# A long convolution and an MLP in one program: four token tiles' first statistics from a second copy of x, and a new total order

## The chip, the cores and the metric

The program runs on one core of one Trainium2 chip. The metric is the device time of one execution in microseconds (us), as the median of several runs. Engines are named as the profile names them: PE (matrix multiply; PEld its weight loads), DVE (vector), ACT (scalar and activations), POOL (GpSimd), SP (sync, which issues most DMAs).

## The reference, cut to what matters

x is `A_q`, 2048 tokens by 640 channels in bf16. All norms are without weights.

```python
h  = x + A(_layernorm(x), k, v, shift_k, ssm_k, ssm_D)
h2 = h + mish(_layernorm(h) @ w1 + b1) @ w2          # w1: 640x1728, w2: 1728x640
# A(q, k, v, ...):
k_shift = causal convolution of k with 4 taps (shift_k), channel by channel
kv = k_shift * v
y  = irfft(rfft(kv, 2S) * rfft(ssm_k, 2S))[:S] + kv * ssm_D
A  = q * y
```

So per channel there is a convolution of length 2048 with a filter of length 2048 (`ssm_k`, one row a channel), whose result is multiplied by the first norm of x and added to x; then a second norm and an MLP with the Mish activation.

## The kernel before, in words

The convolution is a Fourier transform in two stages of matmuls with constant tables. Channels go in 5 groups of 128 (`dc` 0 to 4), tokens in 16 tiles of 128 (`t` 0 to 15). Every step is a small operation object with a name, an engine and its dependencies (`OP`, and `load` for a DMA on SP). Nothing is ordered by a scheduler: the long string `ORDER` lists every operation once, and `_ordered` puts them out in that order, so each engine gets its own operations in the order in which the string has them, and each engine runs its list strictly from first to last. `name@2` gives the PSUM slot (there are four of 128x1024 f32) that a PE operation writes; `:d`, `:p`, `:a` puts an operation on DVE, POOL or ACT instead of its first choice. An operation on PE can start only when the slot's earlier tile was read.

The stages, with the names used in `ORDER` and the profile's lines:

- Filter. `d_n0` to `d_n4` load `ssm_k` (512 KB each, line 328) into the upper part of the big buffer `ks`, from column 20480 on (`raw_n`). `dadd` adds `ssm_D` to the first tap, `k1pe` transposes on PE (L379), `k1ev` copies out of PSUM (L264 on ACT, L266 on DVE: the helper `ev`). `s1kpe` is the first transform stage of the filter (L399, L400; 20 tiles) and `s1kev` the copy out.
- Shift of k. `d_k` loads k; `ktpe` transposes it (L344), `ktev` copies out, `ktsh` shifts a copy on POOL (L348). `d_sk` loads the shift taps (5 KB) by a DMA that ACT issues (L273), `cfpe` spreads them over the partitions with one matmul (L307), `coef` copies that out on DVE (L312), `wsh` makes banded weights of it on POOL (L320), and `kspe` applies them (L360, L361; 10 tiles). `kv` multiplies with v on DVE (L365).
- `s2kpe`, `s2kev` (22 tiles, L425): second stage of the filter, which needs all of `s1kev`. `sw` swaps halves by ten DMAs within `ks` (L453): they write the upper half of `ks`.
- `s1vpe`, `s1vev` (20 tiles), `s2v..pe`, `s2v..ev` (20 tiles): the same two stages for kv. `pr` (20 on DVE, L464) multiplies the spectra. `i1pe`, `i1ev` (20 tiles, L485): first inverse stage. All copies out of PSUM here are casts of 128x1024 or 128x960 on ACT or DVE.
- Per token tile: `i2` (L537) is the last inverse stage, `y` its copy out; `d_x0` to `d_x3` load x into `rb`, where v was; `ln1_t` is the first norm's statistics on DVE (two BATCH_NORM_STATS2 of 320 elements, L516, and an aggregate, L517), `ln1p` the inverse root on POOL, `lnx` the normalised tile; `wb` and `h` multiply and add; `bn`, `pow`, `hc`, `tr` are the second norm and its transposes.
- `m1pe` (L604, L611), `hb` (L626), `m2pe` (L669, L677), `res` (L694), `d_out`: the MLP in five units of tokens.

The x load `d_x` waits for `kv`, since it overwrites v; the statistics wait for `d_x`:

```python
d_x = [load(f"d_x{i}", rb[:, 4 * i * D:4 * (i + 1) * D], ..., deps=[kv_ops[m, i // 2] for m in range(NDC)]) for i in range(4)]
o_ls = OP(f"ln1_{t}", "dve", [d_x[t // 4]], emit=ln1)
cf_pe = OP("cfpe", "pe", [d_cst, d_sk], psum=cf_p, ...)
```

Of the kernel before, what the change touches and what calls it, by code (L numbers as in the profile page):

```python
# [18 lines left out]
D = 640  # L19
# [7 lines left out]
d_dr wz idn d_n0 cz wm@0 small lane d_n1 d_cst d_sk d_n2 warm d_n3 d_n4 d_g0 dsel dcol dadd0 d_k2 k1pe0@1 d_k3 dadd1:p k1pe1@2 d_a12 k1ev0b d_k0 k1ev0  # L27
s1kpe0_3@3 k1ev1 s1kpe0_1@0 s1kev0_3 d_k1 s1kpe0_0@1 dadd2 s1kev0_1 s1kpe1_3@2 s1kev0_0:d dadd3:p d_g4 s1kpe0_2@3 k1pe2@0 s1kev0_2 dadd4:p d_g1
s1kev1_3 kz b1pe@1 k1pe4@3 k1ev2 c_b1 cfpe@2 k1pe3@1 k1ev4:a coef d_v0 s1kpe2_0@0 k1ev3 wsh1 s1kpe2_1@2 s1kev2_0 s1kpe4_3@3 d_g7 s1kev2_1:d s1kpe3_1@1
s1kev4_3 s1kpe2_2@0 wsh3 s1kpe1_0@2 s1kev3_1 d_v1 s1kev2_2:d s1kpe4_1@3 d_g2 s1kev1_0 s1kpe3_2@1 s1kev4_1:d s1kpe1_2@0 s1kev3_2 d_g6 ktpe0_0@2 wsh2  # L30
ktpe0_3 ktpe0_2 s1kev1_2 ktpe2_0@3 ktpe2_3 ktpe2_2 d_v2 ktpe2_1 ktpe0_1 ktev2 ktpe1_0@1 ktev0:a ktpe1_1 ktpe1_3 ktpe1_2 s1kpe3_3@0 d_g5 ktev1 ktsh2
s1kpe4_0@3 s1kev3_3 s1kpe1_1@2 ktsh0 s1kev4_0:d d_v3 s1kpe4_2@1 wsh0 s1kev1_1 s1kpe3_0@0 s1kev4_2:d s1kpe2_3@3 s1kev3_0 d_g3 ktpe4_0@2 ktpe4_2 ktpe4_3
s1kev2_3 ktsh1 ktpe3_0@1 ktpe4_1 ktpe3_3 ktev4 ktpe3_1 ktpe3_2 s2kpe_6@0 s2kpe_12@3 ktev3 s2kev_6 kspe0_0@2 s2kev_12 s2kpe_18@0 kv0_0 ktsh3 kspe2_0@1
s2kev_18 ktsh4 s2kpe_42@3 kv2_0 kspe3_0@2 s2kev_42 s2kpe_96@0 kv3_0 s2kpe_24@1 s2kev_96 kspe4_0@3 s2kev_24 kspe1_0@2 kv4_0 s2kpe_108@0 kspe1_1@1 kv1_0
# [24 lines left out]
d_out5 hb4_3 d_out6 m2pe8@0 m1pe4_0@3 hb4_6 m2pe11@1 hb4_0 res11 m2pe12@3 d_out4 m2pe14@1 res9 m2pe10@2 res12 m2pe13@3 res14 res13 d_out12 d_out14
res10 m2pe15a@1 m2pe15b@3 d_out9 d_out13 d_out10 d_out11 res15a res8 d_out15a res15b d_out8 d_out15b  # L60
# [112 lines left out]
def kernel(  # L173
# [14 lines left out]
    nc = tc.nc  # L188
# [551 lines left out]
```

## Time and profile before

| | |
|---|---|
| median of 3 runs | 222.97 us (222.88 to 223.0) |
| the profiled execution | 223.02 us |
| its span, first to last instruction | 221.2 us, granted PE clock 0.999 |
| busy in the span | PE 212.5 us, DVE 137.6 us, ACT 127.9 us, POOL 62.0 us |

The span is 1.82 us shorter than the profiled execution's own time. Shares over the whole span mix stages with different limits here, so the span is best read in stretches: the filter and the shift of k (to about 28 us), the second stage of the filter between the shift's matmuls (to about 45 us), the transforms of kv and the products (to about 89 us), the first tiles of the last inverse stage (to about 97 us), and the MLP.

### The profile page before, as it was taken

To read this page: it belongs to the slowest core of one execution; us is meant where nothing else is said; L and a number is where in the kernel's file an instruction comes from. 1 tells how busy PE (TensorE), PEld (TensorE's weight loads), DVE (VectorE), ACT (ScalarE), POOL (GpSimd) and SP (SyncE) were. 2 spreads that over 40 slices of the span, in tenths; PEclk is the share of its full clock that TensorE was granted. 3 is DMA by queue.
4 is the path that set the end of the run, shared out by engine and by line. 5 is a ranking of instruction groups with operands and counts; after the bars stand their busy time and mean duration, and the time that the engine had idled before them with its cause. 6 is when DMAs were issued, how large, how long until landed. Compare 5 with 4: busy or idle time off the path is not lost.

```text
span 221.2 us, 6309 instructions
## 1 busy us (share of the span) xinstructions
PE 212.5 (96%) x2740; PEld 156.0 (71%) x2746; DVE 137.6 (62%) x236; ACT 127.9 (58%) x175; POOL 62.0 (28%) x123
## 2 busy tenths in 40 slices
PE   7899999999879999999999999999999999999994
PEld 2899999898769998578867644444567445667663
DVE  2776899999999999899998679920002200002223
ACT  2389888999999999899753038426600257020000
POOL 5147620011870002147988655320000000000000
PEclk9999999999999999999999999999999999999999
DMA  5999994462992690833004402552001100000204
GB/s 168 393 408 416 407 403 109 166 205 87 410 409 92 207 384 9 276 127 77 0 1 27 94 0 59 124 119 59 0 3 59 59 0 3 0 0 3 89 0 148
DMA packets 19564, 30.98 MB, mean 140 GB/s; under 512 B 10705, under 2 KB 14929, under 8 KB 18769
## 3 DMA queue, kind: packets, MB, share of 16 engines
q1 hardware_dynamic: 19104, 30.46, 40.0%
q8 instruction: 21, 0.34, 0.6%
q10 hardware_dynamic: 336, 0.12, 0.2%
q14 instruction: 7, 0.05, 0.1%
q0 software_dynamic: 96, 0.00, 0.0%
HBM read 20.42 MB, written 2.62 MB: 104 GB/s over the span
## 4 chain that ended last, share of the span: by engine, by line
PE 72%; ACT 12%; DVE 6%; DMA 5%; issue 2%; SPq 1%; DVEq 0%; ACTq 0%
PE ps L669 26%; PE ps L604 26%; ACT uv L264 9%; PE ps L537 3%; DMA ks<-ks 3%; PE ps L399 3%; PE ps L425 3%; DMA ks<-in_A_ssm_k_dram 3%; PE ps L344 2%; PE ps L379 2%; DVE ks L266 2%; ACT ks L264 2%; PE ps L360 2%; DVE ra L365 1%; DVE uv L266 1%
## 5 line engine op out<-in xcount | busy, mean ns | idle before, releaser
L626 ACT ACTIVATE ks<-ps,b1s 128x512 bf16<-128x512 f32 (+1 forms) x69 | 36.2, 599 | 44.1 <-PE ps L604 35.1
L669 PE MATMUL ps<-ks 128*128 128x320 bf16 (+2 forms) x420 | 58.6, 299 | 0.0
L604 PE MATMUL ps<-G 128*128 128x512 bf16 (+1 forms) x319 | 57.2, 336 | 0.3
L669 PEld LDWEIGHTS <-ks 128*128 128x128 bf16 x420 | 40.6, 98 | 17.4 <-issue 1.3
L694 DVE TENSOR_TENSOR rb<-ps,rb 128x640 bf16<-128x640 f32 x15 | 11.8, 817 | 64.5 <-PE ps L677 52.2
L604 PEld LDWEIGHTS <-G 128*128 128x128 bf16 x325 | 31.4, 98 | 24.3 <-issue 1.1
L264 ACT CAST ks<-ps 128x960 bf16<-128x960 f32 (+3 forms) x48 | 39.3, 896 | 8.3 <-PE ps L400 5.0
L264 ACT CAST uv<-ps 128x1024 bf16<-128x1024 f32 x46 | 42.6, 1157 | 0.5 <-PE ps L485 0.4
L464 DVE TENSOR_TENSOR ks<-ks,uv 128x2048 bf16<-128x2048 bf16 x20 | 23.4, 1236 | 0.2 <-DMA ks<-ks 0.2
L425 PEld LDWEIGHTS <-G 128*128 128x128 bf16 x512 | 21.0, 96 | 3.1 <-issue 2.5
L485 PE MATMUL ps<-a_t,ks 128*128 128x128 bf16 (+1 forms) x416 | 17.1, 208 | 0.4
L485 PEld LDWEIGHTS <-ks 128*128 128x128 bf16 (+1 forms) x416 | 16.5, 114 | 1.0 <-issue 0.4
L266 DVE CAST uv<-ps 128x1024 bf16<-128x1024 f32 x14 | 16.4, 1210 | 0.2
L530 POOL TENSOR_SCALAR ra<-rb,r,nmr 128x640 bf16<-128x640 bf16 x11 | 12.5, 1133 | 9.9 <-PE ps L400 9.3
L425 PE MATMUL ps<-uv,G 128*128 128x64 bf16 (+1 forms) x384 | 12.9, 187 | 1.7 <-ACT uv L264 1.5
L550 DVE BATCH_NORM_STATS2 st<-rb 128x6 f32<-128x320 bf16 x32 | 14.0, 479 | 0.1
L516 DVE BATCH_NORM_STATS2 st<-rb 128x6 f32<-128x320 bf16 x32 | 13.7, 469 | 0.0
L365 DVE TENSOR_TENSOR ra<-ps,rb 128x1024 bf16<-128x1024 f32 x10 | 11.9, 1222 | 0.7 <-PE ps L361 0.5
L266 DVE CAST ks<-ps 128x1024 bf16<-128x1024 f32 (+2 forms) x10 | 11.3, 1160 | 1.0 <-PE ps L537 0.6
L528 ACT ACTIVATE ra<-rb,nmr,r 128x640 bf16<-128x640 bf16 x5 | 4.5, 925 | 11.9 <-POOL nmr L523 11.9
L425 PE MATMUL ps<-ks,G 128*128 128x160 bf16 x128 | 11.2, 230 | 0.1
L399 PE MATMUL ps<-cst,ra 128*64 128x128 bf16 x160 | 10.6, 219 | 0.7 <-ACT uv L264 0.5
(71 smaller groups left out, 252.7 us busy)
## 6 DMA issues: line engine op xcount, KB each, us to landing
ks<-ks SPq DMA_DIRECT2D x10, 512.0 KB, 6.3
G<-tab_g SPq DMA_DIRECT2D x8, 512.0 KB, 11.1
ks<-in_A_ssm_k_dram SPq DMA_DIRECT2D x5, 512.0 KB, 6.5
ra<-in_A_k_dram SPq DMA_DIRECT2D x4, 640.0 KB, 10.6
rb<-in_A_v_dram SPq DMA_DIRECT2D x4, 640.0 KB, 11.4
rb<-in_A_q_dram SPq DMA_DIRECT2D x4, 640.0 KB, 5.0
out_dram<-rb SPq DMA_DIRECT2D x15, 160.0 KB, 1.8
G<-in_B_w_dram SPq DMA_DIRECT2D x5, 432.0 KB, 5.9
```

The lines of the kernel that those rows point to most:

```text
L264: nc.scalar.copy(o, i)
L266: nc.vector.tensor_copy(o, i)
L365: nc.vector.tensor_tensor(kv_w[:, m, :, 8 * h:8 * h + 8, :], p_.f32().rearrange("p (l t d) -> p d t l", l=4, t=8), raw_v[:, 8 * h:8 * h + ...
L399: nc.tensor.matmul(ps[0:64, dgl, :], lhs, mc, start=True, stop=True)
L425: nc.tensor.matmul(p_.f32()[:, o:o + n], g_v[:, f, :], src[:, :, f, :], start=True, stop=True)
L464: nc.vector.tensor_tensor(o, o, v, ALU.mult)
L485: nc.tensor.matmul(o, KS[r, k, b, :, l], a12[r, k, r], start=k == 0, stop=k == 1)
L516: nc.vector.bn_stats(st1[:, t, hh, :], xt(t)[:, hh * 320:(hh + 1) * 320])
L550: nc.vector.bn_stats(st2[:, t, hh, :], xt(t)[:, hh * 320:(hh + 1) * 320])
L604: nc.tensor.matmul(ph[:, o:o + w], w1[:, dc, fc * P:fc * P + P], lt[:, dc, 0:w], start=dc == 0, stop=dc == NDC - 1)
L626: nc.scalar.activation(hb[:, fc, 0:n], p_.f32()[:, i * 512:i * 512 + n], ACT.Mish, bias=b1s[:, fc:fc + 1], scale=1.0)
L669: nc.tensor.matmul(p_.f32()[:, o:o + n], lhs, w2[:, k, cols:cols + n], start=fc == 0, stop=single and fc == 13)
```

## The change

There are two parts.

First, a new DMA `d_xe` loads the first 2560 columns of x's layout (token tiles 0 to 3, 640 KB) a second time, into `ks` from column 20480 on. That is where the first rows of the filter lay, and it waits for their transposes (`k1pe0` and `k1pe1`). `ln1_0` to `ln1_3` read this copy and no longer wait for `d_x`; `lnx` still reads x in `rb` and now waits for `d_x` itself. The swaps of groups 0 and 1, which overwrite the copy, wait for these four.

Second, `ORDER` is another one throughout: on every engine the operations follow one another differently. The operations themselves are the same but for `d_xe`.

```diff
 ORDER = """
-d_dr wz idn d_n0 cz wm@0 small lane d_n1 d_cst d_sk d_n2 warm d_n3 d_n4 d_g0 dsel dcol dadd0 d_k2 k1pe0@1 d_k3 dadd1:p k1pe1@2 d_a12 k1ev0b d_k0 k1ev0
...
+d_n0 d_n1 wz d_dr idn lane dsel dcol dadd0 d_cst wm@0 d_n2 k1pe0@1 d_n3 dadd1 k1pe1@2 warm k1ev0b s1kpe0_2@3 k1ev0 s1kpe0_3@0 s1kev0_2 small cz
+dadd2:p d_n4 s1kpe0_1@1 k1ev1 d_g0 s1kpe1_3@2 d_k2 k1pe2@3 s1kev0_3:d dadd4 s1kev0_1 d_k3 k1pe4@0 d_a12 b1pe@1 d_k0 d_sk dadd3 s1kev1_3 k1ev2 c_b1
...
+    def xs(t):
+        return ks[:, 20480 + t * D:20480 + (t + 1) * D] if t < 4 else xt(t)
+
...
+    d_xe = load("d_xe", ks[:, 20480:20480 + 4 * D], flat(A_q)[:, 0:4 * D], deps=k1_pes[0:2])
...
-                nc.vector.bn_stats(st1[:, t, hh, :], xt(t)[:, hh * 320:(hh + 1) * 320])
+                nc.vector.bn_stats(st1[:, t, hh, :], xs(t)[:, hh * 320:(hh + 1) * 320])
...
-        o_ls = OP(f"ln1_{t}", "dve", [d_x[t // 4]], emit=ln1)
+        o_ls = OP(f"ln1_{t}", "dve", [d_x[t // 4] if t >= 4 else d_xe], emit=ln1)
+        if t < 4:
+            for o in sw[0] + sw[1]:
+                o.deps.append(o_ls)
...
-        o_lnx = OP(f"lnx{t}", ["act", "pool"], [o_lp] + s1v_in(4096 + t % 9 * D, 4096 + t % 9 * D + D) + ([wbs[t - 9]] if t >= 9 else []), emit=lnxf)
+        o_lnx = OP(f"lnx{t}", ["act", "pool"], [o_lp, d_x[t // 4]] + s1v_in(4096 + t % 9 * D, 4096 + t % 9 * D + D) + ([wbs[t - 9]] if t >= 9 else []), emit=lnxf)
```

What it moves on the engines is shown at two places. The first is the very beginning of ACT's list. Before, ACT issued three DMAs and then began to copy out of PSUM; the third, `sk_r<-in_A_shift_k_dram`, is `d_sk`:

```order
L274 DMA dful<-in_A_ssm_D_dram 128x1x20
L272 DMA cst<-tab_cst 128x416
L273 DMA sk_r<-in_A_shift_k_dram 32x80
L287 ACT_TABLE_LOAD
L287 ACTIVATE warm<-warm 128x2
L264 CAST ks<-ps_64 128x1024
L264 CAST ks<-ps_61 128x1024
L264 CAST ks<-ps_64 128x1024
L264 CAST ks<-ps_63 128x1024
L505 CAST b1s<-ps_62 128x14
L264 COPY ks<-ps_64 128x2048
```

Now the same piece of ACT's list, with the changed kernel's line numbers:

```order
L277 DMA dful<-in_A_ssm_D_dram 128x1x20
L275 DMA cst<-tab_cst 128x416
L290 ACT_TABLE_LOAD
L290 ACTIVATE warm<-warm 128x2
L267 CAST ks<-ps_64 128x1024
L267 CAST ks<-ps_62 128x1024
L276 DMA sk_r<-in_A_shift_k_dram 32x80
L267 CAST ks<-ps_63 128x1024
L509 CAST b1s<-ps_62 128x14
L267 COPY ks<-ps_61 128x2048
```

`d_sk` is now issued behind ACT's first two copies of `s1k` tiles, and ACT copies three such tiles, not four, ahead of `k1ev4` (the COPY of 128x2048). On PE the place of the matmul that needs the taps did not change: `k1pe4`, `b1pe`, `cfpe`, `k1pe3` follow one another in both.

The second place is DVE around the statistics. Before, the first of them stood among the last copies of the filter's second stage and the first of kv's (the other three came later, among the copies of kv's stages):

```order
L266 CAST ks<-ps_63 128x40x24
L266 CAST ks<-ps_61 128x40x24
L516 BN_STATS st_77<-rb 128x6 x2
L517 BN_AGGR mv_78<-st_77 128x2
L365 TENSOR_TENSOR ra<-ps_62,rb 128x32x32
L266 CAST uv<-ps_63 128x1024
L266 CAST uv<-ps_61 128x1024
```

Now three of them stand around the last copies of k's transposes (`uv<-ps` COPY, which are `ktev1`, `ktev3`, `ktev4`) ahead of the first `kv`; the fourth comes after the sixth `kv`. They read `ks`:

```order
L521 BN_AGGR mv_78<-st_77 128x2
L520 BN_STATS st_77<-ks 128x6 x2
L521 BN_AGGR mv_78<-st_77 128x2
L269 COPY uv<-ps_61 128x2x1024
L269 COPY uv<-ps_62 128x2x1024
L269 COPY uv<-ps_63 128x2x1024
L520 BN_STATS st_77<-ks 128x6 x2
L521 BN_AGGR mv_78<-st_77 128x2
L368 TENSOR_TENSOR ra<-ps_64,rb 128x32x32
```

Counted over each engine's list, from `k1ev4` to the last `i1ev`: ACT has 75 copies out of PSUM beside `ktev0` before (10 of `s1k`, 19 of `s2k`, 46 of kv's stages) and 76 now (11, 20, 45). From the first `s1vev` to the last `i1ev` DVE has 15 copies, 20 products, one `kv` and three statistics before, and 16 copies, 20 products and no statistics now. In the `s2k` stage PE's list begins with two `s2k` tiles before the first `kspe` in the kernel before, and with three now; one `s2k` tile (`s2kpe_30`) is left behind the first `s1v` tiles now, two (`s2kpe_90` and `s2kpe_30`) before.

More of the change, by code (lines that the diff above doesn't have):

```diff
@@ L26 @@
 ORDER = """
-d_dr wz idn d_n0 cz wm@0 small lane d_n1 d_cst d_sk d_n2 warm d_n3 d_n4 d_g0 dsel dcol dadd0 d_k2 k1pe0@1 d_k3 dadd1:p k1pe1@2 d_a12 k1ev0b d_k0 k1ev0
-s1kpe0_3@3 k1ev1 s1kpe0_1@0 s1kev0_3 d_k1 s1kpe0_0@1 dadd2 s1kev0_1 s1kpe1_3@2 s1kev0_0:d dadd3:p d_g4 s1kpe0_2@3 k1pe2@0 s1kev0_2 dadd4:p d_g1
-s1kev1_3 kz b1pe@1 k1pe4@3 k1ev2 c_b1 cfpe@2 k1pe3@1 k1ev4:a coef d_v0 s1kpe2_0@0 k1ev3 wsh1 s1kpe2_1@2 s1kev2_0 s1kpe4_3@3 d_g7 s1kev2_1:d s1kpe3_1@1
-s1kev4_3 s1kpe2_2@0 wsh3 s1kpe1_0@2 s1kev3_1 d_v1 s1kev2_2:d s1kpe4_1@3 d_g2 s1kev1_0 s1kpe3_2@1 s1kev4_1:d s1kpe1_2@0 s1kev3_2 d_g6 ktpe0_0@2 wsh2
@@ L31 @@
[L31 to L34, printed above, removed]
@@ new lines @@
+k1ev4:a cfpe@2 k1pe3@3 coef s1kpe1_0@1 s1kpe2_2@2 d_k1 k1ev3 s1kev1_0 s1kpe4_3@0 kz s1kpe3_2@3 s1kev4_3 s1kev2_2:d s1kpe2_0@1 s1kev3_2:d d_g7
+s1kpe4_1@2 d_xe s1kev2_0 s1kpe2_1@0 s1kpe0_0@1 wsh1 wsh0 s1kev4_1 s1kev2_1:d s1kpe3_1@3 s1kpe1_2@2 ktpe0_0@0 ktpe0_3 s1kev3_1:d ktpe0_2 s1kev0_0
+ktpe0_1 s1kev1_2 ktpe2_0@1 ktev0:a wsh3 d_g1 ktpe2_3 ktpe2_2 d_g6 ktpe2_1 s1kpe4_0@3 s1kpe3_0@2 ktev2 s1kpe1_1@0 s1kpe3_3@1 s1kev4_0 s1kpe4_2@3 ktsh2
+s1kev1_1 s1kev3_0:d ln1_2 s1kpe2_3@2 d_v0 s1kev3_3 s1kev2_3 ln1_3 d_g4 ktpe1_0@0 ktpe1_3 ktpe1_2 ktpe1_1 ktpe3_0@1 ktpe3_3 s1kev4_2 ktpe3_1 ktpe3_2
```

54 lines of the change are left out of this document (28 added, 26 removed).

## Prediction, made before the run

> **What bounds the kernel now.** I read the chain of waits first.
>
> ```profile
> PE 72%; ACT 12%; DVE 6%; DMA 5%; issue 2%; SPq 1%; DVEq 0%; ACTq 0%
> ```
>
> PE carries most of it, but not evenly. So I cut the span where ACT changes its work and read the busy times by stretch (length, then PE, PEld, DVE, ACT, POOL).
>
> ```profile
> 15.32:28.13 12.81, 12.77 (x274) 12.01 (x269) 10.03 (x9) 11.12 (x13) 9.28 (x7) 1.00 1.02 414
> 28.13:45.29 17.16, 17.05 (x307) 16.40 (x306) 16.45 (x18) 15.61 (x19) 2.22 (x5) 1.00 0.56 206
> 45.29:89.08 43.79, 40.80 (x1104) 37.81 (x1100) 43.00 (x44) 43.31 (x48) 10.73 (x15) 1.00 0.60 228
> 89.08:97.20 8.12, 7.95 (x64) 4.70 (x64) 7.37 (x20) 7.52 (x13) 1.76 (x4) 1.00 0.86 274
> 97.20:218.67 121.47, 120.70 (x816) 75.12 (x820) 52.87 (x132) 43.19 (x79) 33.22 (x71) 1.00 0.17 40
> ```
>
> From 97.20 us on PE is busy 120.70 of 121.47 us, in both kernels with the same matmuls: that part is PE's. From 45.29 to 89.08 ACT and DVE are both full (43.31 and 43.00 of 43.79), copying tiles out of PSUM and multiplying spectra, and PE waits for slots. So the end of the last `i1ev`, 89.08 us, is set by the copies, and every us won or lost there reaches the end. ACT is the tightest: from the end of `k1ev4` at 15.32 to 89.08, 73.76 us, it works 11.12 + 15.61 + 43.31 = 70.04 and is not busy for 3.72. What it waits for in that time:
>
> ```profile
> ACT ks L264 <- PE ps L425: 2.5, 5, 1.2
> ACT uv L264 <- PE ps L344: 0.5, 1, 0.5
> ACT uv L264 <- PE ps L485: 0.4, 1, 0.4
> DVE uv L266 <- PE ps L344: 1.6, 1, 1.6
> DVE uv L266 <- ACT ks L264: 1.1, 1, 1.1
> DVE ra L365 <- PE ps L361: 0.5, 1, 0.5
> ```
>
> That is 3.4 us of ACT, nearly all of it ahead of 45 us; DVE's 3.2 us lie there too. The change can only win by closing these.
>
> **Part one: the statistics.** One takes two BATCH_NORM_STATS2 and an aggregate.
>
> ```profile
> L516 DVE BATCH_NORM_STATS2 st<-rb 128x6 f32<-128x320 bf16 x32 | 13.7, 469 | 0.0
> L517 DVE BATCH_NORM_AGGREGATE mv<-st 128x2 f32<-128x12 f32 x16 | 3.3, 209 | 0.5
> 42.69 0.88 DVE L516 BATCH_NORM_STATS2 st<-rb 128x6 f32<-128x320 bf16 x2
> 53.45 0.88 DVE L516 BATCH_NORM_STATS2 st<-rb 128x6 f32<-128x320 bf16 x2
> 57.74 0.83 DVE L516 BATCH_NORM_STATS2 st<-rb 128x6 f32<-128x320 bf16 x2
> ```
>
> 2 x 0.469 + 0.209 = 1.15 us each. Three of the four stand in the full stretch (53.45 to 58.8), so 3.4 us of DVE leave it; the new order puts one more cast there (1.15 us, from the next fence but one), so DVE's load falls by about 2.3. They go to the time of DVE's waits of 1.6 and 1.1 us, which they can fill. That is a relief for DVE, not for ACT: the end moves only as far as ACT's list lets it. It is worth nothing alone, and without it DVE would hold ACT's slots.
>
> The copy of x needs 640 KB of a DMA system that is full then. On SP's list 6848 KB (7.0 MB) lie up to and with it; the loads moved 140, 389, 407 and 416 GB/s in the first four stretches of 5 us (0.70, 1.95, 2.04 and 2.08 MB):
>
> ```profile
> 0.00:5.00 5.00, 3.76 (x9) 1.19 (x9) 1.11 (x6) 1.49 (x2) 3.08 (x13) 1.00 0.49 140
> 5.00:10.00 5.00, 4.39 (x91) 3.91 (x92) 2.94 (x6) 0.97 (x2) 0.30 (x1) 1.00 1.02 389
> 10.00:15.00 5.00, 4.81 (x93) 4.52 (x89) 3.53 (x7) 4.41 (x6) 1.05 (x8) 1.00 1.02 407
> 15.00:20.00 5.00, 4.96 (x144) 4.62 (x139) 4.53 (x4) 5.00 (x7) 5.00 (x3) 1.00 1.02 416
> ```
>
> That is 6.77 MB by 20 us, so the copy is there at about 21. DVE has seven copies from `k1ev3` on, which starts near 15, and comes to `ln1_2` at about 24. No wait, then. The tables and v behind it come 1.6 us later (640 KB at 410 GB/s). The tightest is `d_g2`, last in the list now, with 12.9 MB up to it: 6.1 MB more at 410 GB/s, so about 35 us, for an `s2k` tile that PE reaches at 36 by the count below. I take nothing for that.
>
> **Part two: the order, ACT's work.** ACT has one more copy from `k1ev4` to the end (76 for 75). What one costs:
>
> ```profile
> 15.32 5.59 ACT L264 CAST ks<-ps 128x1024 bf16<-128x1024 f32 x6
> 28.13 3.79 ACT L264 CAST ks<-ps 128x960 bf16<-128x960 f32 x4 [1.15 <-PE ps L425]
> 53.43 33.15 ACT L264 CAST uv<-ps 128x1024 bf16<-128x1024 f32 x36
> 54.49 2.30 DVE L266 CAST uv<-ps 128x1024 bf16<-128x1024 f32 x2
> ```
>
> 5.59/6, 3.79/4 and 33.15/36 are 0.93, 0.95 and 0.92 us, so ACT works 0.93 more. Against it stand its waits. Going through PE's new list by hand with 0.41 us for an `s2k` tile, 0.83 for a `kspe` and four slots, PE starts the stage with three `s2k` tiles and then stays ahead of ACT, which has 20 of them in about 17 us of PE's work: of the 2.5 us behind L425 I keep 0.6 (the first tile) and lose 1.9; of the rest I lose 0.5 (L344, where two more copies now stand ahead of `ktev0`) and put 0.4 back for waits I can't see: 2.0 less. `k1ev4` itself ends some 0.2 later, behind `b1pe`. Sum without anything else: 0.93 + 0.2 - 2.0 = **-0.9 us**. Bounds: all 3.7 closed, -2.6; none closed, +1.1. I take -0.9 because the wait rows name the stage and the new list has a reason there.
>
> **Part two: the taps' transfer.** This is what the sum turns on. ACT's first rows and PE's at that time:
>
> ```profile
> 1.40 0.60 ACTq L272 DMA_DIRECT2D cst<-tab_cst  x1
> 2.03 0.45 ACTq L273 DMA_DIRECT2D sk_r<-in_A_shift_k_dram  x1
> 9.03 3.76 ACT L264 CAST ks<-ps 128x1024 bf16<-128x1024 f32 x4 [5.02 <-PE ps L400]
> 13.46 1.87 ACT L264 COPY ks<-ps 128x2048 bf16<-128x2048 bf16 x1 [0.59 <-PE ps L379]
> 12.20 1.22 PE L379 MATMUL ps<-ident,ks 128*128 128x128 bf16 x16
> 13.35 0.20 PE L307 MATMUL ps<-sk_r,cst 32*128 32x80 bf16 x1
> 13.49 1.22 PE L379 MATMUL ps<-ident,ks 128*128 128x128 bf16 x16
> ```
>
> Before, `d_sk` went out at 2.03 and `cfpe` ran at 13.35. Now it goes out behind two casts: 9.03 + 2 x 0.94 = 10.9. PE still comes to `cfpe` at about 13.35 (`k1pe2` and `k1pe4` are bound by `d_n4` and the slots as before). How long a DMA of ACT's takes to land:
>
> ```profile
> cst<-tab_cst ACTq DMA_DIRECT2D x1, 104.0 KB, 4.3
> dful<-in_A_ssm_D_dram ACTq DMA_DIRECT2D x1, 5.0 KB, 2.2
> sk_r<-in_A_shift_k_dram ACTq DMA_DIRECT2D x1, 5.0 KB, 4.9
> ra<-in_A_k_dram SPq DMA_DIRECT2D x4, 640.0 KB, 10.6
> ```
>
> 2.2 us with the DMA engines idle (`dful`, the first); 4.3 with SP's filter loads beside it (`cst`); 4.9 for this very transfer, but behind `cst`. SP's own wait for all that is queued ahead of them: 10.6. At 10.9 the engines are full, and nothing stands ahead on ACT's queue, so I take `cst`'s 4.3: landed at 15.2, `cfpe` at 15.3. PE runs in order, so `k1pe3` and all `s1k` tiles behind it wait too. ACT has `k1ev4` to do until 15.5 and then needs the tile behind `k1pe3`; `cfpe`, `k1pe3` and one tile take 1.85 us, so ACT loses what lies beyond 15.5 - 1.85 = 13.65: 15.3 - 13.65 = **+1.65 us**. ACT is full from there on, DVE's later work shifts alike, and nothing gives it back. Bounds: 2.2 (lands at 13.1) costs 0, 4.9 costs 2.3, 10.6 costs 7.9.
>
> [...]
>
> **Behind 89 us.** From the last `i1ev` to the first `m1pe` (8.12 us) both lists have ten `y` copies and two transposed tiles on ACT and the same DVE row of `wb`, `h`, `bn`, `hc`. `ln1_5`, which now stands ahead of `y0` on DVE, falls where DVE waits for the last tile. I take 0, and 0 for the MLP, bounded by 0.77 either way (121.47 - 120.70, PE's whole idle time there).
>
> **Sum.** -0.9 + 1.65 = +0.75 on the profiled execution of 223.02 (span 221.2, 1.82 around it): 223.8; that execution was 0.05 above the median of the runs shown, so **223.7 us**.
>
> **Rivals.**
> - The taps land before PE needs them (at 13.5 or earlier, 2.6 us after the issue). Then the win of the order shows undiminished: 222.97 - 0.9 = 222.1, **faster**. For it: `dful` took 2.2. Against: the DMA engines were idle then. Chance 0.24.
> - The taps wait for one transfer of SP's in each engine and no more: `dful`'s 2.2 plus 640 KB at 407 GB/s, 1.6 us, lands at 14.7, `cfpe` at 14.8; the loss is 1.15 and the time 223.2, about as before. [...] Chance 0.15.
> - ACT's waits don't close: PE is busy 17.05 of 17.16 us between 28.13 and 45.29, and if it stays the limit there, or a swap or the copy of x comes late to DVE, the one copy more and the later start cost +1.1; with the stall +2.75. 224.1 to 225.7, middle 224.9. Chance 0.13, of which 0.03 for the copy of x landing behind 24 us, when part one doesn't do what it says.
> - The taps wait like SP's own loads, 10.6 us: cost 7.9, time 230. Against it: ACT's transfers overtook SP's. Chance 0.06.
>
> The forecast itself has 0.42, and its own range (landing in 3.7 to 4.9 us, 0.4 either way in ACT's waits) is 222.7 to 224.7.
>
> **Range and chances.** A difference of 0.2% (0.45 us) is about what a measurement of this kernel can tell. Faster holds the first rival (0.24) and a little of the second and the forecast: 0.30. Same holds most of the second and a fifth of the forecast: 0.19. Slower holds the rest: 0.51. The range leaves out the 230 and the best end of the first rival, where all waits close: 221.9 to 225.2.
>
> **What would show it.** Right: `cfpe` (L310 in the changed kernel) starts at about 15.3 with PE idle for 1.9 us ahead of it on the transfer of `sk_r`; ACT idle between `k1ev4` and the next cast; then ACT's waits from there to the last `i1ev` about 2 us in sum instead of 3.7; the statistics at about 24 to 27 us without a wait for the copy. Wrong: `cfpe` on time; ACT still waiting behind L428 (the `s2k` matmuls); a DVE wait for the swaps at the first products; idle PE behind the first `m1pe`.

## The result, and the profile after

The changed kernel takes 231.12 us (230.43 to 231.58, 4 runs) against 222.97 (222.88 to 223.0): a ratio of 1.0363, 95% interval 1.0334 to 1.0393. The direction that had most of the chance was right, the size was not: +8.15 us, where +0.75 was forecast and 225.2 was the end of the range. The profiled execution took 230.81 us, its span 229.0. In all measurements below a run that took over 1.5% longer than the fastest of its kernel is left out of the ratio, which concerns experiment 2 alone.

The chain of waits of the changed kernel has one share that stands out against the one of before: "issue", time in which an engine waited for nothing that the profile shows. It rose from 2% to 5%.

```profile
PE 74%; DVE 9%; ACT 6%; issue 5%; DMA 5%; POOL 0%; SPq 0%; DVEq 0%; POOLq 0%
```

The busy times by stretch, cut at the same events as before (end of `k1ev4`, first copy of an `s2k` tile on ACT, first copy of an `s1v` tile, end of the last `i1ev`, first `m1pe`, last matmul):

```profile
14.41:31.02 16.61, 16.05 (x317) 15.20 (x318) 13.17 (x19) 12.14 (x13) 7.83 (x6) 0.90 1.03 413
31.02:49.08 18.06, 18.06 (x316) 17.64 (x315) 17.22 (x20) 17.19 (x20) 4.20 (x7) 1.00 0.35 126
49.08:96.66 47.58, 41.49 (x1099) 38.73 (x1097) 41.19 (x38) 42.15 (x46) 6.59 (x13) 0.96 0.61 224
96.66:104.55 7.89, 7.41 (x61) 4.31 (x60) 7.70 (x20) 7.09 (x12) 4.79 (x10) 1.00 0.81 270
104.55:226.51 121.96, 121.27 (x824) 75.16 (x821) 53.26 (x132) 43.52 (x79) 33.03 (x68) 1.00 0.19 42
```

Against before the first stretch begins 0.91 us earlier and the five are longer by 3.80, 0.90, 3.79, -0.23 and 0.49: 7.84 us at the last matmul. The first and the third carry it. In both the granted clock (third number from the end; the share of PE's full clock that the chip allowed) is below 1.00, and in the third ACT and DVE are no longer full: 42.15 and 41.19 of 47.58 us.

In the first stretch it is the taps, as foretold. ACT's and PE's rows there in the timeline of the changed kernel, with the idle time ahead of each and what ended it in brackets:

```profile
9.31 0.35 ACTq L276 DMA_DIRECT2D sk_r<-in_A_shift_k_dram  x1
12.54 1.87 ACT L267 COPY ks<-ps 128x2048 bf16<-128x2048 bf16 x1
17.48 1.01 ACT L267 CAST ks<-ps 128x1024 bf16<-128x1024 f32 x1 [3.08 <-PE ps L403]
14.73 0.09 PEld L310 LDWEIGHTS <-cst 32*128 32x128 bf16 x1 [2.39 <-DMA sk_r<-in_A_shift_k_dram]
14.87 1.33 PEld L382 LDWEIGHTS <-ks 128*128 128x128 bf16 x16
```

`cfpe` (L310) started at 14.73, 2.39 us after PE's last weight load ahead of it had ended, and ACT stood for 3.08 us behind `k1ev4`. The transfer took 5.4 us from issue to landing. Then came something that was not foretold; the same columns by stretch as above:

```profile
14.70:16.00 1.30, 1.27 (x15) 1.22 (x16) 0.96 (x4) 0.00 (x0) 0.00 (x0) 0.79 1.02 418
16.00:17.50 1.50, 1.50 (x27) 1.32 (x26) 1.01 (x1) 0.02 (x1) 1.43 (x1) 0.50 1.01 418
17.50:20.00 2.50, 2.50 (x72) 2.50 (x70) 1.87 (x3) 1.88 (x2) 2.50 (x2) 0.73 1.02 418
```

From 15.44 on, just behind the idle time, PE's granted clock was halved (0.50) for 3.4 us: `k1pe3` took 1.33 us instead of 1.08, an `s1k` tile 0.83 to 0.93 instead of 0.48 to 0.50.

In the third stretch PE stood still three times in the middle of a tile, where no semaphore is waited for. PE's weight loads in the changed kernel's timeline around these places:

```profile
57.61 0.11 PEld L402 LDWEIGHTS <-ra 128*64 128x64 bf16 x1 [1.26 <-issue]
65.43 0.72 PEld L428 LDWEIGHTS <-G 128*128 128x128 bf16 x26
69.18 0.17 PEld L428 LDWEIGHTS <-G 128*128 128x128 bf16 x4 [3.03 <-issue]
93.45 0.64 PEld L488 LDWEIGHTS <-ks 64*128 64x128 bf16 x34 [1.07 <-issue]
```

From 66.06 (the last weight load's start) to 69.18 PE started nothing, in the midst of a tile whose slot and inputs it had. From 70.06 on the clock was halved once more for 3.4 us:

```profile
69.20:72.60 3.40, 3.40 (x43) 3.40 (x43) 3.40 (x4) 3.11 (x4) 0.00 (x0) 0.63 0.63 263
```

What ACT waited for between 14.4 and 96.7 us follows from these and from the taps: 10.3 us, where before it was 3.4.

```profile
ACT ks L267 <- PE ps L403: 3.7, 2, 3.1
ACT uv L267 <- PE ps L428: 2.3, 1, 2.3
ACT uv L267 <- PE ps L488: 2.0, 3, 1.1
ACT ks L267 <- PE ps L428: 1.4, 4, 0.7
ACT uv L267 <- PE ps L403: 0.9, 1, 0.9
```

One more thing in the trace happens at these places. Of the changed kernel's DMA queues (packets, MB, share), the one called "instruction" that has 21 packets carries 16 KB in each:

```profile
q8 instruction: 21, 0.34, 0.6%
```

PE executes 2746 weight loads and 2746 matmuls, 5492 instructions, which is 262 for each of the 21 packets. I counted how many of the weight loads were done at each standstill: 991, 1247 and 1756. Between them lie 256 and 509, with their matmuls 512 and 1018 instructions, close to two and four pieces of 256. So I take 256 instructions a packet, an estimate from these counts, divided by 128 (a matmul and its weight load are two instructions, so 128 of each would fill such a piece), and put the packets of this queue beside it. Worked out from the trace's records:

```
changed kernel
packet   starts   lands   PE stands still       weight loads done / 128
  6       55.09   56.04   56.24 to 57.61         7.74
  8       66.77   67.74   66.06 to 69.18         9.74
 12       91.12   92.07   92.27 to 93.45        13.72
packets 15, 16, 18, 20 start when PE is at 15.61, 16.59, 18.60, 20.61 (few other transfers then)
```

In the 2 us ahead of these last four packets the DMA share was 0.34, 0.05, 0.00 and 0.00. So packet n seems to be asked for at about n + 0.6 (an estimate, taken from the quiet places in the last row), and PE stands at about n + 1.74 (7.74, 9.74 and 13.72) if it isn't there; PE goes on 1.4 to 1.6 us after it landed. Measured from n + 0.6, packets 6, 8 and 12 started 3.6, 5.6 and 4.3 us late in the changed kernel, and 2.2, 2.7 and 2.2 us late in the one before, which has no such standstill. From n + 0.6 to their starts the DMA share in the changed kernel was 1.03, 0.89 and 0.91. I take this queue for the fetch of PE's own list of instructions; the trace gives only its name, so this is an inference from the counts and the times above.

That gave three theories, on record ahead of the first four experiments. **T**: the taps' wait carries the whole loss. **F**: late instruction fetches, and the half clock behind each long idle time of PE, carry most of it. **C**: the 640 KB of the second copy in full DMA engines make all behind it late.

### The profile page after: what moved, and what is told of

Same layout as the page of the kernel before. It is cut to its first block, busy times and chain, and to the rows that moved or that the text cites. A ratio compares the mean times of both kernels' runs of the same rounds, so it can differ in the third digit from the quotient of the medians.

```text
span 229.0 us, 6316 instructions
## 1 busy us (share of the span) xinstructions
PE 215.1 (94%) x2746; PEld 158.6 (69%) x2746; DVE 139.0 (61%) x239; ACT 128.4 (56%) x174; POOL 60.0 (26%) x121
## 4 chain that ended last, share of the span: by engine, by line
PE 74%; DVE 9%; ACT 6%; issue 5%; DMA 5%; POOL 0%; SPq 0%; DVEq 0%; POOLq 0%
PE ps L676 25%; PE ps L611 25%; PE ps L428 6%; ACT uv L267 4%; DVE uv L269 3%; PE ps L402 3%; PE ps L488 3%; DMA sk_r<-in_A_shift_k_dram 2%; PE ps L347 2%; DMA ks<-in_A_ssm_k_dram 2%; DVE ks L467 2%; PE ps L363 2%; PE ps L364 1%; PE ps L403 1%; ACT ks L267 1%
## 5 line engine op out<-in xcount | busy, mean ns | idle before, releaser
L269 DVE CAST uv<-ps 128x1024 bf16<-128x1024 f32 x15 | 17.6, 1219 | 6.4 <-PE ps L428 3.1
L488 PE MATMUL ps<-a_t,ks 128*128 128x128 bf16 (+1 forms) x416 | 19.0, 215 | 1.2 <-issue 1.0
L488 PEld LDWEIGHTS <-ks 128*128 128x128 bf16 (+1 forms) x416 | 18.2, 116 | 1.6 <-issue 1.3
L537 POOL TENSOR_SCALAR ra<-rb,r,nmr 128x640 bf16<-128x640 bf16 x11 | 9.5, 869 | 19.4 <-PE ps L403 19.2
L528 POOL TENSOR_SCALAR ve<-mv 128x1 f32<-128x1 f32 x16 | 4.3, 267 | 37.6 <-DVE mv L521 36.9
L557 DVE BATCH_NORM_STATS2 st<-rb 128x6 f32<-128x320 bf16 x32 | 13.8, 475 | 0.2
L402 PE MATMUL ps<-cst,ks 128*64 128x128 bf16 x160 | 11.4, 232 | 0.2 <-ACT ks L267 0.2
L403 PE MATMUL ps<-cst,ks 128*64 128x128 bf16 x160 | 11.4, 234 | 0.0
```

The source lines that it names most:

```text
L269: nc.vector.tensor_copy(o, i)
L402: nc.tensor.matmul(ps[0:64, dgl, :], lhs, mc, start=True, stop=True)
L403: nc.tensor.matmul(ps[64:128, dgl, :], lhs, ms, start=True, stop=True)
L488: nc.tensor.matmul(o, KS[r, k, b, :, l], a12[r, k, r], start=k == 0, stop=k == 1)
L557: nc.vector.bn_stats(st2[:, t, hh, :], xt(t)[:, hh * 320:(hh + 1) * 320])
```

## The experiments

**1. Taps early.** The changed kernel, with `d_sk` where it was:

```diff
-... dadd0 d_cst wm@0 d_n2 ... d_a12 b1pe@1 d_k0 d_sk dadd3 ...
+... dadd0 d_cst d_sk wm@0 d_n2 ... d_a12 b1pe@1 d_k0 dadd3 ...
```

> The changed kernel with one entry of ORDER moved: the taps' transfer d_sk is issued directly behind d_cst again, ahead of ACT's first copy. Theory T (the taps' late transfer carries the whole loss): the 2.4 us wait ahead of cfpe and the half-clock stretch behind it go, and with them nearly all of the 8.1 us: 223 to 224. Theory F (three places where PE stands still in the middle of a tile without waiting for a semaphore, 1.37, 3.12 and 1.18 us long, each at a late fetch of its own instructions, plus the half clock after the longest, carry most): only 2.4 us and 1 to 2 us of half clock come back, 227 to 228.5, and the three gaps are still there, perhaps at other tiles.

Measured: 227.78 us (226.24 to 228.73), ratio 1.0181 [1.0132, 1.0230]. `cfpe` no longer waits, and 3.3 us are back. T falls: 4.8 us stay (4.5 against the 223.27 us that the kernel before took beside it). PE stands still at the same counts as above, 7.74 (1.63 us), 8.74 (0.56), 9.74 (2.17) and 13.72 (0.59). The longest among PE's weight loads:

```profile
66.61 0.18 PEld L428 LDWEIGHTS <-G 128*128 128x128 bf16 x4 [2.08 <-issue]
```

**2. t2m late.** The changed kernel, with the 1 MB load that SP issues ahead of packet 8 put behind `d_w11`:

```diff
-... pr3_0 d_t2m pr3_96 ... d_w11 pr2_32 ...
+... pr3_0 pr3_96 ... d_w11 d_t2m pr2_32 ...
```

> The changed kernel with one entry of ORDER moved: the 1 MB load d_t2m is issued behind the first w1 load (which waits for the last s2v matmul) and no longer directly behind the swaps. Theory F: the fetch that came 5.8 us late beside the swaps and this load comes earlier, the gap of 3.12 us shrinks to under 1.5, no half clock follows, 3 to 5 us come back: 226 to 228. Theory T: the gap has nothing to do with that load, 231 within 1 us.

Measured: 229.66 to 235.01 us in four runs, ratio 1.0343 [1.0268, 1.0417]. The profiled execution is the one of 235.01, so I read only places from it. The standstill at count 9.74 stayed, with packet 8 no earlier. F's special guess, that `d_t2m` makes that packet late, is wrong; what SP issues ahead of that load (a swap, an x load and three swaps from 59.23 to 64.83 us) is enough for it. (The time is T's 231 all the same, but 1 had ruled T out.)

**3. Before, with the taps late.** The kernel before, with `d_sk` behind ACT's first two copies:

```diff
-d_dr wz idn d_n0 cz wm@0 small lane d_n1 d_cst d_sk d_n2 ... s1kev0_1 s1kpe1_3@2 ...
+d_dr wz idn d_n0 cz wm@0 small lane d_n1 d_cst d_n2 ... s1kev0_1 d_sk s1kpe1_3@2 ...
```

> The kernel before with one entry of ORDER moved: d_sk is issued behind ACT's first two copies, as in the changed kernel. Theory T: it costs what the change costs, 8 us: about 231. Theory F: a wait of about 2.4 us ahead of cfpe and some half clock behind it, of which ACT loses 2 to 4 us: 225 to 227, and no gap of over 0.6 us without a semaphore.

Measured: 226.78 us (225.0 to 227.27) beside 223.27 for the kernel before: ratio 1.0144 [1.0096, 1.0193], +3.5 us by the medians. PE and ACT in its timeline, and the stretch behind:

```profile
15.31 0.09 PEld L307 LDWEIGHTS <-cst 32*128 32x128 bf16 x1 [2.43 <-DMA sk_r<-in_A_shift_k_dram]
17.34 1.01 ACT L264 CAST ks<-ps 128x1024 bf16<-128x1024 f32 x1 [2.42 <-PE ps L400]
```

```profile
15.30:19.00 3.70, 3.68 (x69) 3.57 (x71) 2.99 (x6) 1.01 (x1) 2.35 (x2) 0.73 1.01 415
```

`cfpe` ran at 15.31, the very time that the prediction gave for the change. The wait of 2.4 us, and the half clock behind it (0.73 over 3.7 us), cost about twice what the prediction had for the wait alone.

**4. Part one alone.** The changed kernel's code with the order of before; the copy is loaded behind `d_g4`, and its statistics stand where DVE waited:

```diff
+... d_g4 d_xe ... ln1_0 ktev4 ... kv1_0 ln1_1 ... kv4_1 ln1_2 ... s2kev_36:d ln1_3 ...
```

> The code of the changed kernel with the order of before: d_xe is put in behind d_g4, and the four statistics stand early (ln1_0 ahead of ktev4, ln1_1 behind kv1_0, ln1_2 behind kv4_1, ln1_3 where ln1_0 was); d_sk stays first. It tells what the copy and the early statistics do without the new order. Theories T and F both: the copy itself costs little, 222 to 224. A third theory, C (640 KB more in a full DMA stretch is what makes everything late): 225 or more.

Measured: 224.92 us (224.38 to 225.29), ratio 1.0072 [1.0047, 1.0097]: +1.6 us, above T's and F's 222 to 224 and just short of C's 225, so the trace has to decide. Two statistics stand on DVE ahead of a product out of PSUM, and both times PE waits for the slot (from the timeline of this kernel):

```profile
36.10 0.87 DVE L520 BATCH_NORM_STATS2 st<-ks 128x6 f32<-128x320 bf16 x2
38.46 0.22 PE L363 MATMUL ps<-rw,uv 128*128 128x128 bf16 x1 [0.71 <-DVE ra L368]
40.59 0.88 DVE L520 BATCH_NORM_STATS2 st<-ks 128x6 f32<-128x320 bf16 x2
42.85 0.37 PE L428 MATMUL ps<-ks,G 128*128 128x160 bf16 x3 [0.71 <-DVE ra L368]
```

Two waits of 0.71 us are 1.4 of the 1.6. PE has no idle time of over 0.4 us there without a semaphore, and what can be C's is one wait of PE for a table's load, which the kernel before does not have (us in total, times, longest):

```profile
PE ps L428 <- DMA G<-tab_g: 0.4, 1, 0.4
```

C is a small part at most.

**5. Shifted by 58 matmuls.** The sharpest test of F: the kernel of 1 (taps early), with 58 more matmuls at the start of PE's list, whose results nothing reads. A place in the program then comes at another count.

```diff
-        for _ in range(WARM):
+        for _ in range(WARM - 6):
             nc.tensor.matmul(wm_p.f32()[:, 0:512], wz[:, 0:P], wz[:, P:D], start=True, stop=True)
+        for _ in range(64):
+            nc.tensor.matmul(wm_p.f32()[:, 0:64], wz[:, 0:P], wz[:, P:P + 64], start=True, stop=True)
```

> The changed kernel with the taps issued early (227.78 us), and 58 more small PE matmuls at its very start (6 of the 9 long warm-up matmuls replaced by 64 short ones, so PE's idle time there stays as it is). Late fetch (PE stands still because a 256-instruction piece of its own list comes late over full DMA engines): the standstills stay at the same count of PE instructions from the start (pieces 7.74, 9.74, 13.72), so they move 58 matmuls earlier in the program, from tile s1vpe4_2 to about s1vpe2_3 and from s2v1pe_64 to about s2v1pe_96, with other lengths; 225.5 to 228.5 us. Place (something at those tiles stops PE: the swaps' writes, a slot, the buffers): the standstills stay at the same tiles, 1.6 and 2.2 us long; 227.8 us.

Measured: 230.06 us (229.81 to 230.39), ratio 1.0331 [1.0313, 1.0348]. The standstills kept their counts and left their tiles:

```
                 taps early (1)                        shifted by 58 (5)
count 7.74   53.96 to 55.59, in s1vpe4_2        52.46 to 53.78, 58 matmuls earlier in the program
count 8.74   59.85 to 60.41                     57.79 to 59.43
count 9.74   64.44 to 66.61, in s2v1pe_64       63.50 to 66.99, 58 matmuls earlier in the program
elsewhere    90.80 to 91.39 (13.72)             18.40 to 19.29 (2.74), 24.92 to 25.58 (3.74), 92.57 to 93.58 (14.72)
```

The longest of them in the timeline of the shifted kernel, and its queue, which has one packet more for 116 instructions more:

```profile
63.08 0.52 PEld L430 LDWEIGHTS <-G 128*128 128x128 bf16 x18
66.99 0.42 PEld L430 LDWEIGHTS <-G 128*128 128x128 bf16 x14 [3.39 <-issue]
```

```profile
q8 instruction: 22, 0.36, 0.7%
```

The place in the program is out; the count decides. The time went beyond F's range (228.5), since F had not reckoned with longer standstills: packets 7 and 8 start 5.0 and 7.4 us late (4.0 and 4.9 in 1).

**6. Swaps late.** The kernel of 1, with `s2kpe_30` and its copy, for which the swaps wait, six `s1v` tiles later:

```diff
-... s1vpe3_1@1 s2kpe_30@0 s1vev0_2:d ... s1vev1_1 s2kev_30:d ... s1vpe2_1@2 s1vev0_1:d ...
+... s1vpe3_1@1 s1vev0_2:d ... s1vev1_1 ... s1vpe2_1@2 s2kpe_30@0 s1vev0_1:d s2kev_30:d ...
```

> The changed kernel with the taps early (227.78 us), and the last tile of the filter's second stage (s2kpe_30 and its copy) six s1v tiles later, so that the ten swaps, which wait for it, start at about 52.5 us instead of 48.6. Late fetch: the piece of PE's list that came at 53.3 now goes out ahead of the swaps, so the standstill of 1.6 us in s1vpe4_2 is gone; the one of 2.2 us in s2v1pe_64 stays or moves, as the DMA engines are full there all the same; 225 to 227 us. Place: standstills as before or 4 us later with the swaps; 227.8 us or more, since the first products wait for the swaps.

Measured: 225.96 us (225.25 to 226.59), ratio 1.0141 [1.0114, 1.0168]. Packet 6 now starts 1.8 us late instead of 4.2, and the standstill at 7.74 is gone; the one at 9.74 is 1.63 us instead of 2.17, and no half clock follows it in the profiled execution. (At 51.22 PE stands for 1.32 us for the slot of `s2kpe_30`, a wait of this edit's own.) F, as expected.

**7. Swaps spaced, in name.** The kernel of 1, with each swap made to depend on the third ahead of it in the list of dependencies:

```diff
+    for a, b in zip(sw_q, sw_q[3:]):
+        b.deps.append(a)
```

> The changed kernel with the taps early (227.78 us), and each swap waiting until the third swap ahead of it has landed, so that at most three of the 512 KB swaps are in flight instead of about six. Late fetch: what the fetch waits for is the transfers queued ahead of it on its DMA engine; with half of them queued it comes within 3 us, the standstills in s1vpe4_2 and s2v1pe_64 shrink under 0.7 us each and the half clock behind the second is gone; 224 to 226 us, if no product waits for a late swap. Place: both standstills stay; 227.8 us or more.

Measured: 227.88 us (227.23 to 229.03), ratio 1.0233 [1.0202, 1.0264]. The edit did nothing: SP issued seven swaps in 7.47 us as in 1 (7.56), since that list only states the order, and what is waited for follows from the data. So it tells nothing of the spacing, nor of what a fetch is queued behind, which was a guess; as a second measurement of the program of 1 it gives nearly the same time (227.78 there) and the standstills at the same counts (7.74, 8.74, 9.74).

**8. Paced.** The kernel of 1, with the swaps and three x loads in groups, each behind a DMA of 8 bytes that reads what a chosen copy has written, so that SP waits there:

```diff
+    OP("pc0", "sp", [s1["v", 2, 2][1]], emit=lambda e: nc.sync.dma_start(pace_t[0:1, 0:4], uv[0:1, 10744:10748]))
...
+... s1vev2_2 pc0 sw0_1 sw0_0 sw1_1 ... s1vev3_3 pc1 sw1_0 sw2_1 sw2_0 ... s2v0ev_96 pc2 sw3_1 sw3_0 sw4_1 ... s1vev4_3 pc3 sw4_0 d_x1 ... s2v2ev_48 pc4 d_x3 d_x2 ...
```

> The changed kernel with the taps early (227.78 us), its ten swaps and three loads of x in five groups of two or three, each group behind a tiny DMA that SP can issue only when a named copy has written what it reads (about 51, 55, 59, 64 and 75 us), so that each 256-instruction piece of PE's list (asked for at about 48, 53, 58, 62 and 71 us) meets few transfers. Late fetch: no standstill of over 0.7 us without a semaphore in s1vpe4_2 and s2v1pe_64, no half clock there; 222 to 224.5 us. Place, or the swaps' traffic as such: standstills as in the kernel with early taps; 227 to 229 us. If the first products wait for a swap, DVE shows a wait for a DMA of ks.

Measured: 226.35 us (224.93 to 227.02), ratio 1.0127 [1.0081, 1.0173]. Packets 6 and 8 start 1.6 and 3.0 us late, and the standstills at 7.74 and 9.74 are gone (0.64 us are left at 8.74). But the transfers that were moved back, with `d_t2m` and `w1` behind them, now meet packet 12, 5.2 us late, and at 13.72 PE stands for 2.2 us; half clock follows (from 87.86 on):

```profile
87.92 1.20 PEld L488 LDWEIGHTS <-ks 64*128 64x128 bf16 x43 [2.06 <-issue]
```

So the time missed F's range (224.5) by a standstill that moved on with the transfers.

**9. Before, shifted by 58.** The kernel before, with the edit of 5:

> The kernel before with 58 more small PE matmuls at its start (6 of 9 long warm-up matmuls replaced by 64 short ones). Late fetch: that the kernel before has no standstill is a matter of where its pieces of 256 instructions fall against the transfers; moved by 58 matmuls, one or two of them fall into the swaps (53.6 to 66 us) at another point and at least one standstill of 0.5 to 2 us appears, always at a count of n + 0.74; 223.5 to 226.5 us. Place: nothing at the start matters later; 222.6 to 223.2 us.

Measured: 226.34 us (225.89 to 226.96), ratio 1.0143 [1.0117, 1.0170]. 58 idle matmuls more at the start cost 3.2 us, with nothing else changed. Two standstills appear, at counts 2.74 and 7.74; PE's weight loads behind them:

```profile
19.93 0.11 PEld L401 LDWEIGHTS <-ks 128*64 128x64 bf16 x1 [1.41 <-issue]
54.16 0.11 PEld L401 LDWEIGHTS <-ra 128*64 128x64 bf16 x1 [1.40 <-issue]
```

Set side by side, the records of the two traces show that hardly anything else is in it. From 8.8 us to the first standstill each weight load of the program starts within 0.01 us of its time in the kernel before (18.411 beside 18.408 us for the last one). The next one is 1.50 us late, the one behind the second standstill 3.06, and the last of the program 2.99; the two profiled executions differ by 2.97 us. That the kernel before has no standstill is how its list falls against its transfers.

**10. Paced throughout.** The kernel of 8, with `d_t2m` and the five loads of `w1` in three more groups:

```diff
+... s2v1ev_0 pc5 d_t2m ... i1ev3_3 pc6 d_w11 d_w10 d_w12 ... i1ev2_1:d pc7 d_w13 d_w14 ...
```

> The paced kernel (226.35 us) with the loads behind the swaps spread too: the tables t2m and the five of w1 in three groups behind tiny DMAs at about 77, 82 and 87 us, so that the piece of PE's list asked for at about 80 us meets an empty queue. Late fetch: the one standstill left (2.2 us in i1pe4_3, count 13.72) and the half clock behind it go; 222.3 to 224 us, about the kernel before. Whether the new order is the better one without its standstills is then to be read: under 222.5 it is. If the paced loads come too late, PE waits at the first i2 or m1 matmul for a DMA of t2m or w1, and it is 224 to 226.

Measured: 222.79 us (222.54 to 223.49, 12 runs) beside 222.88, ratio 0.9995 [0.9982, 1.0007]. Packets 5 to 12 start 0.8 to 3.5 us late, the longest standstill without a semaphore is 0.7 us (at 13.72), and the clock is 1.00 in every stretch. The 5.0 us between 1 and this kernel, whose lists for PE are the same, are the price of the late fetches and the half clock behind them. Its stretches, cut as above, and ACT's waits from 14.4 to 88.5 us:

```profile
14.83:27.65 12.82, 12.77 (x284) 12.02 (x279) 11.35 (x15) 12.04 (x13) 7.07 (x6) 1.00 1.02 413
27.65:45.72 18.07, 18.07 (x316) 17.65 (x315) 17.23 (x20) 17.19 (x20) 4.20 (x7) 1.00 0.54 204
45.72:88.41 42.69, 40.11 (x1099) 37.00 (x1097) 41.54 (x38) 41.96 (x46) 6.60 (x13) 1.00 0.62 224
88.41:96.47 8.06, 7.59 (x61) 4.35 (x60) 7.86 (x20) 7.26 (x12) 4.96 (x10) 1.00 1.00 351
96.47:218.26 121.79, 120.79 (x815) 75.19 (x820) 53.06 (x131) 43.34 (x79) 32.86 (x68) 1.00 0.19 45
```

```profile
ACT ks L267 <- PE ps L428: 1.4, 4, 0.7
ACT uv L267 <- PE ps L488: 0.6, 1, 0.6
```

**11. t2m earlier.** The kernel of 10, with `d_t2m` behind `pc4`, two x loads among those of `w1`, and one group less:

```diff
-... s2v2ev_48 pc4 d_x3 d_x2 ... s2v1ev_0 pc5 d_t2m ... i1ev2_1:d pc7 d_w13 d_w14 ...
+... s2v2ev_48 pc4 d_t2m ... i1ev2_1:d pc6 d_x2 d_w13 d_w14 d_x3 ...
```

> The wholly paced kernel (222.79 us, one standstill of 0.7 us left at count 13.72) with t2m issued at about 72 us instead of 78 and the last two loads of x among the loads of w1 at about 87, so that nothing is in flight when the piece of PE's list for that place is asked for at about 79. Late fetch: the 0.7 us go; 222.0 to 222.7 us, under the kernel before by up to 0.4%. If that standstill cost nothing, or the loads of w1 come late to the first MLP matmuls: 222.7 to 223.5 us.

Measured: 222.46 us (222.13 to 224.05, 12 runs) beside 223.0 (222.72 to 223.76), ratio 0.9994 [0.9974, 1.0014]. The standstill at 13.72 is gone, and seven runs lie between 222.13 and 222.48, below every run of the kernel before; five lie between 222.96 and 224.05. That it is faster is not shown.

**12. The new order without part one.** The kernel of 10 without the second copy, its four statistics reading x in `rb` as before; I chose places for them among the `s1v` copies:

```diff
-... d_xe ... ln1_2 ... ln1_3 ... ln1_1 ... ln1_0 ...
+... s2kev_30:d ln1_2 ... s1vev1_0 ln1_0 ... s1vev0_1:d ln1_3 ... s1vev1_2:d ln1_1 ...
```

> The wholly paced kernel (222.79 us) without part one: no second copy of x, and the four statistics read x where v was, among the copies of kv's stages, 4.6 us of DVE's work there. What the prediction said of part one (worth something only in that it keeps DVE from holding slots that ACT's work needs): 223.5 to 226 us. Part one worth nothing: 222.4 to 223.2 us. Part one a loss, as in the order of before: 221 to 222.3 us.

Measured: 227.31 us (226.44 to 229.64), ratio 1.0202 [1.0160, 1.0244]: 4.5 us more than 10. PE's waits between 46 and 60 us in its trace, four of the five behind a statistic:

```profile
PE ps L399 <- DVE uv L266: 3.9, 5, 1.0
```

The profiled execution took 229.64 us, and 2.2 us of its excess over kernel 10 are there at 9.8 us already, so only the waits are read from it. In this order, and at these places, the copy is worth about what the four statistics take of DVE (4 x 1.15 us). The prediction's reading of part one, that without it DVE would hold slots, holds; the range given for it (up to 226) was too low.

## Why the prediction was wrong, by its own steps

- **The taps.** Mechanism right, size too small. The issue was at 9.31 (10.9 foretold), the landing 5.4 us later (4.3), `cfpe` at 14.73 (15.3). By the prediction's own sum ACT would have lost 14.73 - (14.41 - 1.85) = 2.2 us; it stood for 3.08, because `k1pe3` and the tile behind it ran at half clock, and stood 0.62 more at the next tile. The term of +1.65 us measured 3.3 (experiment 1) and 3.5 (experiment 3). What the sum left out is the half clock behind the idle time.
- **"From 45.29 to 89.08 ACT and DVE are both full ..."**, so that the end of the last `i1ev` is set by the copies. True of the profile before, and the main step that failed in the forecast: it lets PE wait for slots and semaphores alone. PE also stood still behind packets that I take for its own instructions, which started 3.6, 5.6 and 4.3 us late in the changed kernel, at a DMA share of 0.89 to 1.03. The new order lets SP begin the swaps 3.2 us behind the first `s1v` tile (at 47.69 on PE) where before it was 9.5 (at 44.11), as the rows of SP below show, so that packet 6 too falls among them. The prediction asked of each transfer only who waits for its data. That is 5.0 us (1 against 10), two thirds of the miss of 7.4 (231.1 - 223.7); the rest is 1.65 of the taps' term and some 0.8 of the next. With the taps alone the time would have been some 226 (kernel 10's 222.79 and 3.3), an estimate: slower, as forecast, and for the reason given, but outside the range too.

The swaps on SP's list in the changed kernel, then in the one before:

```profile
50.91 7.74 SPq L456 DMA_DIRECT2D ks<-ks  x7
```

```profile
53.64 10.83 SPq L453 DMA_DIRECT2D ks<-ks  x10
```

- **"What it waits for"**, -0.9 us. In kernel 10 ACT's waits from `k1ev4` to the last `i1ev` are 2.0 us, as I had it for the change, and the last `i1ev` ends at 88.41 instead of 89.08: -0.67. At the last matmul 0.41 is left (218.26 against 218.67), the MLP taking 121.79 instead of 121.47. In the medians it is 0.09, which can't be told from nothing. The gain that was to be measured is at most a small one.
- **Part one, "worth nothing alone".** In the order of before it costs 1.6 us (4); in the new order, going without it costs 4.5 (12). What I had as filling of DVE's waits is a question of place: a statistic just ahead of an operation that frees a slot was a wait of PE's (two of 0.71 us in 4). In the changed kernel the copy landed 10.8 us after its issue, and all four statistics ran without waiting for it, as foretold (they began at 27.1 to 41.3, later than the 24 to 27 foretold, the first of them by the taps' delay, since in kernel 10 it is at 23.8).
- **Behind 89 us**: 0 taken; 7.89 against 8.12 us to the first `m1pe`, 121.96 against 121.47 behind it, inside the 0.77 us.
- **The rivals.** None was what happened. The second, the taps behind one transfer of SP's in each engine (landing 3.8 us after the issue), is ruled out by 5.4 and, in experiment 3, 6.2 us. Its condition, that one transfer and no more, was a guess that no run here shows; the instruction packets, on a queue of their own too, started up to 7.4 us late (5, packet 8), where it gives a wait of 1.6.

The two amounts, 3.3 us for the taps and 5.0 for the late fetches with their half clock, are differences of medians one after the other, so they add up to the loss by their making. The traces check them apart from that. The changed kernel and kernel 10 have the same list for PE, so the start of each weight load can be set beside its like (worked out from the records; count as above, changed kernel less kernel 10):

```
count                                             us
1.07   ahead of cfpe                           -0.45
1.08   cfpe                                    +2.01
2.34   behind the half clock                   +3.36, and the same to 0.01 us until 7.73
7.74   behind the first standstill             +4.71
9.73   ahead of the longest                    +4.30 (kernel 10 stands still for 0.4 at 8.74)
9.74   behind it                               +7.17
13.71  behind the half clock                   +7.77
13.72  behind the last standstill              +8.25, and the same at the last matmul
```

So the taps with their half clock carry 3.4 us here and the fetches with theirs 4.9. Kernel 10, without either, stands 0.1 below the kernel before.

Not settled: what in the DMA engines makes a packet wait. Packet 12 started 4.3 us late in the changed kernel and 2.2 in the one before, with 1728 and 1888 KB of SP's transfers issued and not yet landed when PE stood at 12.6 (worked out from the traces); 7 told nothing of the spacing. Nor is it settled whether part one and the order could be told apart at better places for the statistics.

## What to carry to other kernels

The long unrolled list of short matmuls was, by the counts here, itself a stream of loads. PE ran through 256 instructions in 4.5 to 5.6 us between the counts 6 and 10 (kernel before), and the standstills of the changed kernel came where the DMA share was 0.89 to 1.03. In a kernel like this one, look for idle PE with no releaser in the midst of a tile, and count instructions to see whether it returns at a fixed step. Keeping large transfers that nothing needed yet out of such stretches, by a wait that paces them, was worth 5.0 us here (1 against 10); an edit ahead, even of idle matmuls, moved the standstills, and cost 1.4% (9). And a small load that PE needs early is worth issuing ahead of the copies on its engine: its wait, with the half clock that it brought, cost 3.3 us here (1).

## What the runs showed of the hardware

- The queue "instruction" brought 21 packets of 16 KB beside 5492 matmuls and weight loads of PE, 262 each, and 22 beside 5608 (5), 255 each; 256 is the estimate from the distances of the standstills. A packet was asked for about 1.14 pieces (some 146 matmuls) ahead of need, an estimate from n + 0.6 and n + 1.74, and PE went on 1.2 to 1.6 us after it landed. That is so of all 26 standstills of 0.5 us or more at a count of n + 0.72 to n + 0.74 in ten traces (that of 2 left out); at other counts no idle time as long was without a semaphore or a slot that ended it. Standstills of over 1 us followed starts that were 3.6 to 7.4 us late, but for one of 1.02 us with a start only 2.1 us late (5, at 14.72), where PE ran through the 146 matmuls in 3.6 us instead of the 4.6 at 7.74.
- Half clock came with single idle times of PE of 2.17, 2.18, 2.48, 2.58, 2.72, 3.12 and 3.49 us (from one weight load's start to the next), and with no single one of 1.02 to 1.66 us. But it also came in the profiled execution of kernel 12, behind two of 1.29 us, from 55.90 and from 58.02:

```profile
57.00:60.00 3.00, 1.78 (x46) 1.64 (x47) 2.96 (x6) 1.20 (x2) 2.37 (x7) 0.87 0.62 251
60.00:62.00 2.00, 2.00 (x39) 1.83 (x36) 0.95 (x2) 1.01 (x1) 1.52 (x2) 0.50 1.03 430
```

  Together they are 2.58 of the 3.41 us from 55.90 to 59.31, so the length of one idle time does not decide alone; no run here settles what does. In kernel 1 the half clock began at 65.68, when PE had been idle for only 1.24 us of the 2.17, while in 7 PE stood for 1.66 us in one piece and kept its clock. It lasted 3.4 us (15.44 to 18.86 and 70.06 to 73.47 in the changed kernel), in kernel 1 6.8.
- A load of 5 KB on ACT's queue (`d_sk`) landed 5.4 us after its issue while SP's loads moved 407 GB/s (changed kernel, 9.31 to 14.70), 6.2 in experiment 3, and 4.9 behind `cst` (kernel before); another one, `dful`, 2.2 us after its issue at 0.73, with a DMA share of 0.00 until 2.10 and 0.84 from there to 2.95.
